# A recurrent scan gated by a GLU: x and the weights in four slots of 128 rows, with the halves of the array trading banks between two turns

## The chip, the cores and the metric

One core of a Trainium2 chip. Its engines run side by side: TensorE (PE, with its weight loads as PEld), VectorE (DVE), ScalarE (ACT), GpSimd (POOL) and SyncE (SP, which only issues DMAs here). The metric is the device time in microseconds, as the median of several runs; smaller is better. Matmul results land in PSUM, which has eight banks of 512 fp32 columns; only DVE and ACT copy from there.

## The reference

Tokens S = 2048, width D = 448, hidden width F = 1792, all bf16. The part that matters here:

```python
xn = layernorm(x)                                   # [2048, 448]
Bu = einsum("bld,pd->blp", xn, B_bar)               # complex, B_bar from Lambda, log_dt, B
h  = Lam_bar * h + Bu[:, t, :]                      # scan over 2048 tokens
s  = 2 * einsum("blp,dp->bld", hseq, Cmat).real + xn * Dskip
g  = einsum("bsd,df->bsf", xn, w_gate)
u  = einsum("bsd,df->bsf", xn, w_up)
gl = einsum("bsf,fd->bsd", sigmoid(g) * u, w_down)
out = x + s * silu(gl)
```

## The kernel before, in words

The tokens go in four chunks of 512 (four tiles of 128 each). The width 448 is seven blocks of 64 rows, so it does not fill a whole number of 128-row contractions. The kernel therefore splits PE's array in two halves of 64 rows. For one gate or up unit (`gu_mm`, L800) the upper half contracts all seven blocks for one column block of the weights into one bank, while the lower half does the same for another column block into a second bank. Seven pairs of matmuls make a unit of 2 x 128 columns by 512 tokens:

```python
T.matmul(bank[0][:, ts], lhsT=w_[0:H, s, ms], rhs=x[0:H, SL[s], ts], start=(s == 0), stop=(s == 6))       # L810
T.matmul(bank[1][:, ts], lhsT=w_[H:P, (s + 1) % 7, ms], rhs=x[H:P, SL[s], ts], ...)                       # L811
```

For this both halves need all 448 rows: `xnT` has seven slots in which the 128 partitions hold 64 rows each for either half, and every row lies there twice. The normalized tile is therefore widened by a copy of its own columns on POOL (in `norm`, L541) before it is transposed; in chunk 0 the tiles are transposed on PE, copied by ACT into four slots (`first_slots`, L593) and the rest is filled by DVE from SBUF (`shift`, L600). Weights `wG` and `wU` lie with one half of their columns in partitions 0 to 63 and the other in 64 to 127, and each DMA fills 64 partitions.

A unit's two banks are one of three `gu` tiles, taken in turn (`next_gu`). After a gate unit ACT takes the tanh of both banks (L844), after an up unit DVE multiplies (L847). The last two banks are `acc0` and `acc1`, for the down and output products and the fourth part of the B product.

The B product (`b_phase`, L873) has four parts for each chunk. It uses three full 128-row contractions (L899, L902) and one half-row pair (L885, L888). Its results go by ACT (L913, L919) to `bus` buffers, and DVE does the scan from them. In chunks 1 to 3 the down products (L1027) and output products (L1046) of earlier chunks stand between the B product's third and fourth part.

The order of each engine is not written out by hand alone: every operation goes with a cost into a planner (`Plan`), PE in the order written, DVE and ACT in the written order in the head (`pl.seq`) and afterwards by due times. DMA issues keep their written order on each queue; eight DMA semaphores are reused in turn, so an issue can wait for an earlier DMA's landing. In the head DMAs are issued from SP, ACT and POOL.

The head: ten warm-up matmuls; statistics of the first tiles on DVE and ACT, roots on ACT (`root`, L485), `norm` on DVE (L531); transposes; then the first two gate units in four pieces of 128 tokens (`last_tile`, L828 and L829), one for each tile as it comes. From there on units have 512 columns; `halves` cuts the first two of chunk 1 in pieces of 256.

Of the kernel before, what the change touches and what calls it, by code (L numbers as in the profile page):

```python
# [15 lines left out]
ENG = mybir.EngineType  # L16

# [229 lines left out]
def kernel(  # L247
# [36 lines left out]
    wgt = {"g": sbt("wG", [7, 896]), "u": sbt("wU", [7, 896])}  # L284
# [3 lines left out]
    xn = [sbt(f"xn{i}", [2 * D]) for i in range(NXN)]  # L288
    SL = [4 * s % 7 for s in range(7)]
    xnT_raw = [sbt(f"xnT{i}", [7 * L]) for i in range(3)]  # L290
    xnT = [flat(t[:], 7, L) for t in xnT_raw]
# [6 lines left out]
    bT6 = sbt("bT6", [4, P])  # L298
# [48 lines left out]
    gu = [pp.tile([P, 2, 512], FP32, name=f"gu{i}") for i in range(3)]  # L347
    acc = [pp.tile([P, 512], FP32, name=f"acc{i}") for i in range(2)]
# [17 lines left out]
    def load_w(eng, k, half, b, r=(), rate=105e3, land=0.0):  # L366
        m0, m1 = BLK[k][b]
        ps = slice(half * H, half * H + H)
        c0 = half * 896
        load(eng, [("w", k, half, m) for m in range(m0, m1)], H * 7 * (m1 - m0) * P * 2,  # L370
             wgt[k][ps, :, m0 * P:m1 * P],
             wsrc[k][:, c0 + m0 * P:c0 + m1 * P].rearrange("(s p) f -> p s f", p=H), cost=0.65, r=r, rate=rate, land=land)

    def load_w0(eng, half, part, r=(), land=0.0):
        ps = slice(half * H, half * H + H)
        s0, c0 = (1 - half if part == "A" else half), half * 896
        n = 4 - s0
        load(eng, [("w", "g", half, m, part) for m in range(2)], H * n * 2 * P * 2, wgt["g"][ps, s0:7:2, 0:2 * P],
             wsrc["g"][:, c0:c0 + 2 * P].rearrange("(s p) f -> p s f", p=H)[:, s0:7:2, :], cost=0.5, r=r, rate=400e3, land=land)

    def wkeys(k, m, part=None):
        if k == "u" or m > 1:
            return [("w", k, 0, m), ("w", k, 1, m)]
        if part == "b":
            return [("w", k, 0, m, "A"), ("w", k, 1, m, "A")]
        return [("w", k, h, m, q) for h in range(2) for q in "AB"]
# [14 lines left out]
    def load_p(eng, k, r=()):  # L401
# [3 lines left out]
    load_x(2, 1, "SP", land=3.7)  # L405
    load_x(1, 1, "ACT", land=3.5)
    add("ACT", 0.05, lambda: A.preload_act_table_set("sqrt_and_others"), w=["sqrttab"], lat=1.3, chain=True)
    load_x(3, 1, "ACT", land=4.3)
    load_w0("SP", 0, "A", land=5.7)
    load_w0("ACT", 1, "A", land=5.9)  # L410
    load_w0("SP", 0, "B", land=6.4)
    load_w0("SP", 1, "B", r=[("x", 0)], land=6.6)
# [5 lines left out]
    load_w("SP", "g", 0, 1, rate=400e3, land=8.5)  # L418
    load_w("SP", "g", 1, 1, rate=400e3, land=9.5)
    load_w("SP", "g", 0, 2, rate=400e3, land=11.0)  # L420
    load_w("SP", "g", 1, 2, rate=400e3, land=12.4)
    load_x(4, 2, land=13.6)
    load_x(6, 2, land=15.1)
# [7 lines left out]
    add("POOL", 0.15, lambda: G.memset(flat(g_raw[:, 512:2048], 3, 512)[:, :, D:512], 0.0),  # L431
        w=[("xnw", t) for t in (1, 2, 3)])
    load_w("SP", "u", 0, 0, rate=400e3, land=16.3)
    load_w("SP", "u", 1, 0, rate=400e3, land=18.2)
    load_w("SP", "u", 0, 1, rate=400e3, land=19.4)
    load_w("SP", "u", 1, 1, rate=400e3, land=20.5)
    load_w("SP", "u", 0, 2, rate=400e3, land=21.6)
    load_w("SP", "u", 1, 2, rate=400e3, land=22.7)
# [9 lines left out]
    def bn(t):  # L448
        b = t % 3
        add("DVE", 0.56 if t < TPC else 0.6, lambda: V.bn_stats(out=bst[b][:], in_=x_all[:, t, :]),  # L450
            r=[("x", t)] + ([("xnT", 0, 3, "a")] if 3 < t < 8 else []), w=[("bst", b)])
# [74 lines left out]

    def norm(t):
        b, o = xkey(t), xbuf(t)
        if t < TPC:
            s1, op0 = (nmf[:, 1, :], ALU.add) if t == 1 else (mvf[:, t, 0:1], ALU.subtract)  # L530
            add("DVE", 0.33, lambda: V.tensor_scalar(out=o[:, 0:448], in0=x_all[:, t, :], scalar1=s1,  # L531
                                                     scalar2=rsd[:, t, :], op0=op0, op1=ALU.mult),
                r=[("x", t), ("mv", t), ("rs", t)], w=[("xn", b)])
        else:
            add("ACT", 0.65, lambda: A.activation(o[:, 0:448], x_all[:, t, :], ACT.Identity,  # L535
                                                 bias=nmr[:, t, :], scale=rsd[:, t, :]),
                r=[("x", t), ("rs", t), ("nm", t)], w=[("xn", b)])
        n = H if t < TPC else D
        if 0 < t < TPC:
            return  # L540
        add("POOL", 0.25 if n == H else 0.6, lambda: G.tensor_copy(out=o[:, D:D + n], in_=o[:, 0:n]),  # L541
            r=[("xn", b)], w=[("xnw", b)])

    def skip_row(t):
        b, q, o = xkey(t), t % NXD, xbuf(t)
        add("DVE", dve2(448), lambda: V.tensor_tensor(out=xd[q][:], in0=o[:, 0:448], in1=dbc[:], op=ALU.mult),
            r=[("xn", b), "dbc"], w=[("xd", q)])
# [3 lines left out]
    def next_acc():  # L551
        a = acc_n[0] % 2
        acc_n[0] += 1
        return a

    def xkeys(c):
        return [("xnT", c % 3, j) for j in range(TPC)]

    def pe_transpose(t, parts, between=None):
        b, js, o = xkey(t), slice(t * P, t * P + P), xbuf(t)  # L560
        tp = {}
        for lo, hi, key, bank, eng in parts:
            for s in range(lo, hi):
                tp[s] = flat(bank.bitcast(BF16)[:, 0:(hi - lo) * P], hi - lo, P)[:, s - lo, :]

        def f():
            for s in (4, 5, 6, 0, 1, 2):
                c0 = s * P if s < 4 else H + (s - 4) * P
                T.transpose(tp[s], o[:, c0:c0 + P], ident[:, :])
        add("PE", 0.64 if t < 2 else 0.34, f, r=[("xn", b), "ident"], w=[p[2] for p in parts])  # L570
        add("PE", 0.1 if t < 2 else 0.06, lambda: T.transpose(tp[3], o[:, 384:512], ident[:, :]), r=[("xnw", b)], w=[parts[-1][2]])
        for i, (lo, hi, key, bank, eng) in enumerate(parts):
            if i and between:
                between()
            n = (hi - lo) * P
            w = [("xnT", 0, t, h) for h in (("a" if lo == 0 else "b") if len(parts) == 2 else "ab")]
            src = flat(bank.bitcast(BF16)[:, 0:n], hi - lo, P)
            if eng == "ACT":
                add("ACT", 0.05 + n / 1120.0, lambda src=src, lo=lo, hi=hi: A.copy(out=xnT[0][:, lo:hi, js], in_=src), r=[key], w=w)
            else:  # L580
                add("DVE", 0.07 + n / 1600.0, lambda src=src, lo=lo, hi=hi: V.tensor_copy(out=xnT[0][:, lo:hi, js], in_=src), r=[key], w=w)

    def first_slots(t, key, bank, eng):
        b, js, o = xkey(t), slice(t * P, t * P + P), xbuf(t)
        tp = flat(bank.bitcast(BF16)[:, 0:512], 4, P)

        def f():
            for s in range(3):
                T.transpose(tp[:, s, :], o[:, s * P:s * P + P], ident[:, :])
            T.transpose(tp[:, 3, :], o[:, 384:512], ident[:, :])  # L590
        add("PE", 0.24, f, r=[("xn", b), ("xnw", b), "ident"], w=[key])
        cost, e = (0.51, A.copy) if eng == "ACT" else (0.39, V.tensor_copy)
        add(eng, cost, lambda: e(out=xnT[0][:, 0:4, js], in_=tp), r=[key], w=[("xnT", 0, t, "a")])  # L593

    def shift(t, half, eng):
        js = slice(t * P, t * P + P)
        dst, src = ((slice(0, H), slice(4, 7)), (slice(H, P), slice(0, 3))) if half == 0 else (
            (slice(H, P), slice(3, 7)), (slice(0, H), slice(0, 4)))
        cost, e = (0.45, A.copy) if eng == "ACT" else (0.32, V.tensor_copy)
        add(eng, cost, lambda: e(out=xnT[0][dst[0], dst[1], js], in_=xnT[0][src[0], src[1], js]),  # L600
            r=[("xnT", 0, t, "a")], w=[("xnT", 0, t, half)])
        if half == 0:
            add("NONE", 0.0, lambda: None, r=[("xnT", 0, t, 0), ("xnT", 0, t, 1)], w=[("xnT", 0, t, "b")], lat=0.0)

    def dma_transpose(t):
# [4 lines left out]
        tload([k + ("a",), k + ("b",)], xnT[c % 3][:, :, js], o, P * 1792, r=[("xn", b), ("xnw", b)] + al)  # L610

    def xr(c, lo=0, hi=TPC):
        return [("xnT", c % 3, j, h) for j in range(lo, hi) for h in "ab"]
# [50 lines left out]
    def silu_table():  # L664
        add("ACT", 1.3, lambda: A.preload_act_table_set("silu_and_others"), r=[("sd", t) for t in range(4)] + [("xnT", 0, 3, "a"), "pv0"], w=["silutab"])
# [519 lines left out]
    for i in range(4, 13):  # L1185
        gu_step(0, i)
# [82 lines left out]
```

## Time and profile before

| what | value |
|---|---|
| median of 3 runs | 183.17 us (183.04 to 183.57) |
| the profiled execution's own time | 183.15 us |
| its span, first to last instruction | 181.4 us |
| around the span | 1.75 us |
| granted TensorE clock | 1.00 |
| PE / DVE / ACT / POOL busy | 176.9 / 166.5 / 97.4 / 35.2 us |

How to read it: the page's first part gives busy time, share of the span and number of instructions of each engine. The second cuts the span in 40 slices of 4.5 us and gives tenths of busy time in each, and what the DMAs moved. A timeline line gives start and duration in microseconds, engine, line of the kernel, operation, what it writes and reads, and in brackets how long the engine was idle before and what ended that. In a line of the waits view stand the total, the number and the longest of the waits of one line for another. PE's duration of a matmul is its whole passage, not its spacing; the spacing is read from starts.

### The profile page before, as it was taken

How to read it: one execution, taken by the hardware profiler on the slowest of the kernel's cores; microseconds unless marked ns; L12 is line 12 of the kernel's file. 1: busy time of each engine (PE TensorE's matmuls, PEld its weight loads, DVE VectorE, ACT ScalarE, POOL GpSimd, SP SyncE). 2: the span in 40 equal slices, each digit the busy share in tenths (PEclk: the TensorE clock that was granted, in tenths of full speed). 3: DMA queues.
4: the chain of work that ended last, by engine and by line, in shares of the span. 5: the costliest groups of instructions: out<-in, count | busy, mean ns of one | idle time of the engine just before them, and what ended most of it. 6: DMA issues, size and time to landing. Idle time of an engine off the chain costs nothing.

```text
span 181.4 us, 3610 instructions
## 1 busy us (share of the span) xinstructions
PE 176.9 (98%) x1404; PEld 89.0 (49%) x1411; DVE 166.5 (92%) x294; ACT 97.4 (54%) x160; POOL 35.2 (19%) x93
## 2 busy tenths in 40 slices
PE   8999999999999999999999999999999999999993
PEld 2755555654544444455554444444555444455552
DVE  3768889999989999999999999999999999999772
ACT  4899998867699984464155543348110533411100
POOL 6464483000018785000004100000000000000000
PEclk9999999999999999999999999999999999999999
DMA  4999999998000390000004900002000000002111
GB/s 122 245 224 228 183 157 203 291 217 248 4 0 0 62 145 0 0 4 0 0 2 91 131 9 0 4 0 73 3 4 0 25 27 28 1 0 76 50 62 47
DMA packets 30852, 13.43 MB, mean 74 GB/s; under 512 B 19441, under 2 KB 30834, under 8 KB 30834
## 3 DMA queue, kind: packets, MB, share of 16 engines
q1 hardware_dynamic: 30208, 12.83, 35.0%
q10 hardware_dynamic: 562, 0.36, 0.7%
q8 instruction: 11, 0.18, 0.5%
q14 instruction: 7, 0.06, 0.1%
q0 software_dynamic: 64, 0.00, 0.0%
HBM read 6.77 MB, written 1.84 MB: 47 GB/s over the span
## 4 chain that ended last, share of the span: by engine, by line
PE 94%; DMA 2%; DVE 1%; ACTq 0%; issue 0%; ACT 0%; DVEq 0%
PE gu L810 36%; PE gu L1027 15%; PE acc L1046 11%; PE acc L1027 9%; PE gu L899 8%; PE gu L811 8%; DMA wG<-in_B_w_gate_dram 2%; PE acc L902 2%; PE gu L885 2%; PE gu L828 2%; PE acc L810 1%; ACTq L357 0%; DVE o_t L1088 0%; PE gu L829 0%; DVE o_t L1082 0%
## 5 line engine op out<-in xcount | busy, mean ns | idle before, releaser
L810 PE MATMUL gu<-xnT,wU 64*128 64x512 bf16 x196 | 45.8, 376 | 0.0
L811 PE MATMUL gu<-xnT,wU 64*128 64x512 bf16 x196 | 45.8, 376 | 0.0
L811 PE MATMUL gu<-xnT,wG 64*128 64x512 bf16 (+1 forms) x189 | 41.3, 360 | 0.0
L810 PE MATMUL gu<-xnT,wG 64*128 64x512 bf16 (+1 forms) x189 | 41.3, 360 | 0.0
L844 ACT ACTIVATE sig<-gu 128x1024 f32<-128x1024 f32 x21 | 21.3, 1019 | 24.7 <-PE gu L811 20.2
L1027 PEld LDWEIGHTS <-hF 128*128 128x128 bf16 x224 | 21.9, 98 | 20.6
L1027 PE MATMUL gu<-wd,hF 128*128 128x448 bf16 x140 | 28.0, 352 | 0.0
L810 PEld LDWEIGHTS <-wG 64*128 64x128 bf16 x196 | 18.3, 94 | 17.5
L810 PEld LDWEIGHTS <-wU 64*128 64x128 bf16 x196 | 18.4, 94 | 17.1
L847 DVE SCALAR_TENSOR_TENSOR hF<-sig,gu 128x1024 bf16<-128x1024 f32 x21 | 25.4, 1210 | 0.7 <-ACT sig L844 0.4
L1046 PE MATMUL acc<-cT,hT 128*128 128x448 bf16 (+2 forms) x119 | 22.9, 337 | 0.0
L966 DVE TENSOR_TENSOR_SCAN wv<-c_r,st,z 128x512 bf16<-128x512 f32 x18 | 22.8, 1271 | 0.0
L811 PEld LDWEIGHTS <-wU 64*128 64x128 bf16 x196 | 18.4, 94 | 5.2
L1033 ACT ACTIVATE g_t<-gu 128x448 bf16<-128x448 f32 x10 | 5.4, 540 | 27.7 <-PE gu L1027 16.8
L811 PEld LDWEIGHTS <-wG 64*128 64x128 bf16 x196 | 18.3, 94 | 2.3 <-DMA wG<-in_B_w_gate_dram 0.3
L1027 PE MATMUL acc<-wd,hF 128*128 128x448 bf16 x84 | 16.9, 352 | 0.0
L1046 PEld LDWEIGHTS <-hT 128*128 128x128 bf16 x126 | 11.7, 98 | 9.9 <-issue 0.4
L899 PE MATMUL gu<-xnT,bT 128*128 128x512 bf16 x65 | 15.3, 379 | 0.4
L913 ACT CAST bus<-gu 128x1024 bf16<-128x1024 f32 x12 | 12.0, 1011 | 5.9 <-PE gu L885 5.3
L541 POOL COPY xn<-xn 128x448 bf16<-128x448 bf16 x12 | 7.5, 626 | 28.9 <-ACT xn L535 28.7
L919 ACT CAST bus<-acc 64x256 bf16<-64x256 f32 (+1 forms) x24 | 8.7, 368 | 5.1 <-PE acc L902 4.8
L450 DVE BATCH_NORM_STATS2 bst<-x_all 128x6 f32<-128x448 bf16 x11 | 6.4, 612 | 4.8 <-DMA x_all<-in_A_x_dram 4.8
(162 smaller groups left out, 262.4 us busy)
## 6 DMA issues: line engine op xcount, KB each, us to landing
wd<-in_B_w_down_dram SPq DMA_DIRECT2D x2, 784.0 KB, 6.7
out_dram<-o_t SPq DMA_DIRECT2D x14, 112.0 KB, 1.7
wU<-in_B_w_up_dram SPq DMA_DIRECT2D x4, 224.0 KB, 8.8
x_all<-in_A_x_dram SPq DMA_DIRECT2D x2, 448.0 KB, 4.1
wG<-in_B_w_gate_dram SPq DMA_DIRECT2D x2, 336.0 KB, 7.1
wU<-in_B_w_up_dram SPq DMA_DIRECT2D x2, 336.0 KB, 7.8
wG<-in_B_w_gate_dram SPq DMA_DIRECT2D x2, 224.0 KB, 5.4
x_all<-in_A_x_dram SPq DMA_DIRECT2D x2, 224.0 KB, 7.9
```

Source lines behind the costliest of these rows:

```text
L450: add("DVE", 0.56 if t < TPC else 0.6, lambda: V.bn_stats(out=bst[b][:], in_=x_all[:, t, :]), r=[("x", t)] + ([("xnT", 0, 3, "a")] if 3 < ...
L541: add("POOL", 0.25 if n == H else 0.6, lambda: G.tensor_copy(out=o[:, D:D + n], in_=o[:, 0:n]), r=[("xn", b)], w=[("xnw", b)])
L810: T.matmul(bank[0][:, ts], lhsT=w_[0:H, s, ms], rhs=x[0:H, SL[s], ts], start=(s == 0), stop=(s == 6))
L811: T.matmul(bank[1][:, ts], lhsT=w_[H:P, (s + 1) % 7, ms], rhs=x[H:P, SL[s], ts], start=(s == 0), stop=(s == 6))
L844: add("ACT", act(1024), lambda: A.activation(th, gu[a][:], ACT.Tanh, scale=0.5), r=[("gu", a)], w=[tk])
L847: add("DVE", dve1(1024), lambda: V.scalar_tensor_tensor(out=ho, in0=th, scalar=1.0, in1=gu[a][:], op0=ALU.add, op1=ALU.mult), r=[("gu", a) ...
L899: T.matmul(gu[slots[pt]][:, i, :], lhsT=bT[:, kt, i, pt * P:pt * P + P], rhs=x[:, kt, :], start=(first and kt == 0), stop=(not first and k ...
L913: add("ACT", act(1024), lambda: A.copy(out=bus[u][:], in_=gu[slots[pt]][:]), r=key(pt), w=[("bus", u)])
L919: add("ACT", 0.36, lambda ns=ns, d=d, q=q, l=l, i=i: A.copy(out=bus[u][d, l, ns], in_=acc[a3[i]][q, 0:256]), r=[("acc", a3[i])] + ([("bus" ...
L966: dve(1.194, lambda k=k: V.tensor_tensor_scan(out=wv[:, k, :], data0=rb, data1=z[:, k, :], initial=(st[pt][:, k, :] if c else 0.0), op0=AL ...
L1027: T.matmul(d, lhsT=hF[c % 2][:, m, h, js], rhs=wd[:, ft, :], start=(ft == 0), stop=(ft == FT - 1))
L1046: T.matmul(y, lhsT=hT[c % 2][:, hm, js], rhs=cT[:, cm, c0:c1], start=(i == 0 and not skip_on_pe), stop=(i == 6))
```

## The change

x and the weights are laid out in four slots of 128 rows: rows 0, 128, 192 and 320 onward. The upper half of the array then has blocks 0, 2, 3 and 5 of the seven, the lower half blocks 1, 3, 4 and 6; block 3 is in both. Each half multiplies its own rows for both column blocks. A unit is one pair for block 3 (`z_mm`: each half for its own bank), three pairs of the first turn (`ph_mm` with i = 0, same banks) and three of the second turn (i = 1), in which the halves trade banks. Before a half writes a bank that the other half wrote, PE waits for that product. The second turn of a unit is put behind the first two pairs of the next one (`run_unit`, `flush`); in the pieces (`both`) two units alternate. The ring gets `acc` as a fourth tile. The B product is done in the same way, with no 128-row matmuls. The POOL copies and the DVE shifts go; chunk 0's tiles 1 to 3 are transposed by each half for itself (`row_transpose`), with one copy on ACT and one on DVE. `norm` writes 512 columns in two overlapping pieces of 256. Weight DMAs fill 128 partitions with rows of 512 or 768 columns; the first weights come in four DMAs, two from SP and two from ACT. The rows of `wd` are taken in another order to match.

```diff
-    wgt = {"g": sbt("wG", [7, 896]), "u": sbt("wU", [7, 896])}
+    wgt = {"g": sbt("wG", [4, F]), "u": sbt("wU", [4, F])}
-    xn = [sbt(f"xn{i}", [2 * D]) for i in range(NXN)]
+    xn = [sbt(f"xn{i}", [4 * P]) for i in range(NXN)]
+    LO, UP = (slice(0, H), (0, 1, 3), 2), (slice(H, P), (0, 2, 3), 1)
+    gu = [pp.tile([P, 2, 512], FP32, name=f"gu{i}") for i in range(4)]
+    acc = [gu[3][:, i, :] for i in range(2)]
...
+    load_w0("SP", 0)
+    load_w0("ACT", 1)
+    load_w0("SP", 2)
+    load_w0("ACT", 3)
...
     def norm(t):
-        n = H if t < TPC else D
-        if 0 < t < TPC:
-            return
-        add("POOL", 0.25 if n == H else 0.6, lambda: G.tensor_copy(out=o[:, D:D + n], in_=o[:, 0:n]),
...
+    def row_transpose(t, keys, banks):
+            for s in range(4):
+                for h, (hs, _, _) in enumerate((LO, UP)):
+                    T.transpose(tp[h][:, s, :], o[hs, s * P:s * P + P], ident[hs, hs])
+    def row_copy(t, h, key, tp):
+        js = slice(t * P + h * H, t * P + h * H + H)
+        eng, cost, e = (("ACT", 0.33, A.copy), ("DVE", 0.25, V.tensor_copy))[h]
...
+    def row_mm(bank, h, fn, start=False):
+        pe_n[0] += 1
+        other = None if start else wrote.get((bank, 1 - h))
+        if start:
+            wrote.pop((bank, 1 - h), None)
+        if other and other[0] > seen[0]:
+            tc.add_manual_dep(T.nop().ins, other[1].ins.name, SYNC, reason="other rows' product in this bank")
+            seen[0] = other[0]
+        wrote[bank, h] = (pe_n[0], fn())
+    def z_mm(u, start):
+            for b, (hs, _, s) in enumerate((LO, UP)):
+                row_mm(banks[b], b, lambda: T.matmul(out[b], lhsT=w(b, hs, s), rhs=x(b, hs, s), start=start, stop=False), start)
+    def ph_mm(u, i, qs=(0, 1, 2), start=False, stop=False):
+            for q in qs:
+                for h, (hs, ss, _) in enumerate((LO, UP)):
+                    b = 1 - h if i else h
+                    row_mm(banks[b], h, lambda: T.matmul(out[b], lhsT=w(b, hs, ss[q]), rhs=x(b, hs, ss[q]),
+                                                         start=start and q == 0, stop=stop and q == 2), start and q == 0)
+    def flush():
+        if open_unit:
+            u, done = open_unit.pop()
+            ph_mm(u, 1, stop=True)
+            done()
+    def run_unit(u, done):
+        n0 = 1 if u[6] == L else 3
+        z_mm(u, True)
+        ph_mm(u, 0, range(n0))
+        flush()
+        if n0 < 3:
+            ph_mm(u, 0, range(n0, 3))
+        open_unit.append((u, done))
+    def both(us, first=False, last=False, between=None):
+        if first is None:
+            z_mm(us[0], True)
+            flush()
+            z_mm(us[1], True)
+        for u in us:
+            ph_mm(u, 0, start=first is True)
+        if first is not None:
+            for u in us:
+                z_mm(u, False)
+        if between:
+            between()
+        for u in us:
+            ph_mm(u, 1, stop=last)
...
     def b_phase(c, mid=None):
-        for pt in (3, 0, 1):
-            add("PE", ..., lambda pt=pt: fulls(pt, False), ...)
-            evac(pt)
+        for pt in (3, 0, 1, 2) if c else (0, 1, 3, 2):
+            run_unit(unit(pt), lambda pt=pt: evac(pt))
         if mid:
             mid(...)
+            flush()
-        add("PE", 1.29, lambda: fulls(2, True), ...)
-        add("PE", 0.22 + SW, lambda: halfrows(2, False), ...)
-        evac(2)
```

## The prediction

> **What bounds the kernel now.** I read four views in this order. First the page's busy line and slices, to see which engine is full:
>
> ```profile
> PE 176.9 (98%) x1404; PEld 89.0 (49%) x1411; DVE 166.5 (92%) x294; ACT 97.4 (54%) x160; POOL 35.2 (19%) x93
> PE   8999999999999999999999999999999999999993
> GB/s 122 245 224 228 183 157 203 291 217 248 4 0 0 62 145 0 0 4 0 0 2 91 131 9 0 4 0 73 3 4 0 25 27 28 1 0 76 50 62 47
> ```
>
> PE is full in every slice but the first and last. A busy PE need not be fast, so the second view is PE's waits:
>
> ```profile
> PE gu L444 <- PEq L1253: 0.8, 1, 0.8
> PE gu L829 <- DMA wG<-in_B_w_gate_dram: 0.3, 1, 0.3
> ```
>
> After the first product PE waits once, 0.3 us for weights. Third, PE's timeline at the end of the gate/up work, for the spacing:
>
> ```profile
> 155.71 0.38 PE L810 MATMUL gu<-xnT,wU 64*128 64x512 bf16 x1
> 155.71 0.38 PE L811 MATMUL gu<-xnT,wU 64*128 64x512 bf16 x1
> 155.92 0.38 PE L810 MATMUL gu<-xnT,wU 64*128 64x512 bf16 x1
> ...
> 156.35 0.38 PE L810 MATMUL gu<-xnT,wU 64*128 64x512 bf16 x1
> ...
> 156.66 0.93 PE L1046 MATMUL acc<-cT,hT 128*128 128x448 bf16 x4
> ```
>
> L810 and L811 start together: the two halves run as a pair, and pairs follow each other every 0.215 us. From the last pair to the first 128-row matmul there is 0.31 us: 0.095 more, which I call a **switch**. From 10.34 us, where the 512-column units begin, to the last matmul, the starts hold nothing else beyond matmul counts times spacing (some records are missing). So the kernel is a head of 10.34 us and then PE's list. Only the head, the length of the list, or a new PE wait can move the time. Fourth, the head's timeline:
>
> ```profile
> 1.74 0.41 ACTq L357 DMA_DIRECT2D x_all<-in_A_x_dram  x1
> 2.19 0.70 ACTq L357 DMA_DIRECT2D wG<-in_B_w_gate_dram  x1
> 3.81 0.30 ACT L485 ACTIVATE sdb<-mvf,epsc 128x1 bf16<-128x1 f32 x1 [0.82 <-DVE mvf L456]
> 4.37 0.36 DVE L531 TENSOR_SCALAR g_t<-x_all,mvf,rsd 128x448 bf16<-128x448 bf16 x1
> 5.23 0.36 DVE L581 COPY xnT<-acc 128x384 bf16<-128x384 bf16 x1
> 5.64 0.22 PE L828 MATMUL gu<-xnT,wG 64*128 64x128 bf16 x1
> 6.11 0.23 PE L829 MATMUL gu<-xnT,wG 64*128 64x128 bf16 x1 [0.25 <-DMA wG<-in_B_w_gate_dram]
> 6.98 0.59 ACT L593 COPY xnT<-gu 128x512 bf16<-128x512 bf16 x1 [0.42 <-PE gu L590]
> 10.34 0.38 PE L810 MATMUL gu<-xnT,wG 64*128 64x512 bf16 x1
> ```
>
> To be seen: the chain root (3.81), norm (4.37), transpose, copy (5.23), product. From 6.11 to 10.34 PE is nearly closed: 55 pairs of 128 columns at 0.056 (starts at 8.50, 8.55 and 8.61 in the same view) and 12 transposes at about 0.056 make 3.75 of the 4.23 us.
>
> **The change part by part.**
>
> *PE's list after the head.* Gate/up: seven pairs for each unit before and after (one that both halves do of the middle 64 rows, and 3 + 3 turns). The B product was six 128-row matmuls and one pair; it becomes seven pairs, at the same spacing. Two switches go, those of chunk 0's B product, where nothing of 128 rows is left: 2 x 0.095 = **-0.2 us**. Weight loads do not bind: in the 128-column stage a pair with its two loads took 0.056.
>
> *The new wait at each turn.* In the changed program as built, 89 weight loads on PE wait for PE's own semaphore: a half may enter a bank only after the other half's last product there is complete. Behind such a load everything on PE is queued. Price: ACT at L844 in the window around 70 us was waiting for PE, the unit's last pair started at 69.74 and ACT at 70.16, so a 512-column product is out 0.42 us after its start. In a steady unit two pairs stand between (z and the first turn's first pair of the next unit), so the matmul behind the wait is due at 3 x 0.215 = 0.645. That leaves 0.22 for a load of 0.09. I take **0**; the bounds are no gain and, if each of the some 62 steady turns lost as much as a switch, 62 x 0.095 = 5.9 us. Nearest is the row of 0.42, so 0. In the half-tile units (`halves`) there is less between: one 256-column pair after chunk 0's B product (due at 0.33, wants 0.43: 0.1), one after each 256-column z (0.1), and small change at the end of chunk 3: **+0.25** in all, 0 to 0.5.
>
> *The head.* Three things count here.
>
> (a) ACT now issues the fourth piece of the first weights, and as built that issue waits for the semaphore of x tile 1 before it can take it over. x tile 1 is issued at 1.30 and lands 2.5 us later (the page's DMA issues: x_all on ACTq, median 2.5), about 3.85. The issue takes 0.4 (row at 1.74). The root of tile 0 is the next instruction on ACT, so it starts at 4.3, not 3.81. Behind it hang norm, transpose, copy and PE: **+0.5**. The norm writes 512 columns instead of 448 (+0.05), the copy takes 512 rather than 384 (+0.1) and waits for four transposes, not three (+0.05). The distance from root to first product was 5.64 - 3.81 = 1.83, so the first product starts at 4.3 + 1.83 + 0.2 = 6.35. Before, PE was held by the weights until 6.11, so only 0.25 of this shows. The fourth piece, issued at 3.9 behind two larger transfers on SP's queue, lands at 6.1 to 6.5 and is wanted two pairs later: no wait of its own.
>
> (b) Self-waits with little between. In a 128-column tile the order is turn 1 of units 0 and 1, z of 0, z of 1, turn 2 of 0. After z of 0 only one pair stands between: due 0.11 after its start, ready at 0.25 to 0.3 (L590 starts at 6.73, ACT at 6.98). I take 0.16, and 0.05 for the passage to the next tile. Three tiles pay the first (in tile 1 the transposes of tile 3 stand between), two the second: about 0.6.
>
> (c) Tile 1's columns. Before, its copy ran beside tile 0's second half. Now the transposes follow all of tile 0, then ACT copies one half (256 columns: 0.37, as L919), and as built the DVE copy of the other half waits for ACT (about 0.25), and PE for both. Tile 0 ends at 6.35 + 14 x 0.056 + 0.16 = 7.3; transposes to 7.5; out at 7.7; ACT to 8.1; DVE to 8.4; PE resumes at 8.45, with 0.7 idle (tile 2's transposes take 0.2 of that hole). Tile 1: 8 pairs, tile 3's transposes, 6 pairs: 1.0, to 9.45. Tiles 2 and 3: 0.05 + 0.78 + 0.16 each, to **11.45**.
>
> So the 512-column units begin at 11.45 instead of 10.34: **+1.1**. Gone in exchange are DVE's six shifts (L600, 1.9 us) and ACT's wide copies. Neither engine ended a PE wait, so that is worth nothing itself; nor are POOL's copies (7.5 us) and the smaller DMA transposes, as those columns lay ready before PE came.
>
> *Weights.* One seventh more bytes, in 128 partitions instead of 64. In the slices, the 64-partition loads ran at 224 to 245 GB/s, the down weights (128 partitions, slice 8) at 291. I take the latter: no wait. At 228 GB/s, with the lag of about 2 us that the landings showed, the third gate block would come at 14.3 for a need at 13.8, and I allow 0.5. [...]
>
> *Buffers.* Two units are open at once, and acc joins the ring as a fourth: usually 3.45 us from a unit's end to the bank's next start (3.0 before), but 1.94 where only three may be used, and the fourth unit of chunks 2 and 3 must now leave its bank within 2.7 us; before, DVE did it at 88.3, ten us late. Copies out took 1.5 to 2.7 us from the unit's end. I take 0; up to 1.5 if DVE comes late.
>
> **Sum**, on the profiled execution of 183.15 us (span 181.4 and 1.75 around it; the median is 183.17): 183.15 + 1.1 - 0.2 + 0.25 = **184.3 us**. Without (a), 0.25 less.
>
> **Rivals.**
> *The head closes up.* x tile 1 lands earlier and the copies hide: PE starts near 6.1 and runs 56 pairs and 12 transposes with no hole, 6.1 + 3.1 + 0.7 = 9.9. That is -0.45; with -0.2 and +0.25, 182.75. For it: 0.48 of the old head is waits and switches that could go. Against: ACT's order as built and the DVE-after-ACT copies.
> *The turn's wait bites.* This is the firm slower case: if the release of a waiting load takes over 0.13 us longer than ACT's, each of 62 turns is late; at a switch's 0.095 each, +5.9, 190. Against: the spare 0.22. The trace of before has no PE wait on PE.
> *Late evacuation.* DVE, 100% busy from 80 to 170 us, holds a bank: +1 to 1.5, 185.5. For it: the slack of 1.94 and 2.7 against copies of 1.5 to 2.7. Against: in the old trace PE never waited for DVE.
> *It nets out:* (a) does not show, and the hole before tile 1 shrinks to the 0.2 that tile 2's transposes fill: 184.3 - 0.25 - 0.5 = 183.55. For it: landings move by some tenths. Against: both holes follow from the order as built.
>
> **How the numbers follow.** A measurement of this kernel can tell about 0.3%, 0.55 us. Forecast 0.50; late evacuation 0.11; the turn's wait 0.08; nets out 0.12; the head closes up 0.19. Faster 0.19, same 0.13, slower 0.68. The range takes in the closed head (182.75, and without the half tiles' 0.25, 182.5) and late evacuation with the bounds of the weights and half tiles (186.0); outside lie the turn's wait and tails.
>
> **What would show it.** The first 512-column unit at 11.4 (the closed head: 9.9); tile 0's root at 4.3 behind ACT's DMA issue; PE idle 0.4 to 0.7 between tiles 0 and 1; pairs still every 0.215 across turns; from the first 512-column pair to the end, 171.0 before, 171.1 after. A gap at every turn, or PE waiting for DVE or ACT after 20 us, would make it wrong.

## The result and the profile after

The changed kernel takes **193.84 us** (median of 4 runs, 193.37 to 194.05); the kernel before took 183.19 beside it (183.04 to 183.57). The ratio is 1.0574, with a 95% interval of 1.0548 to 1.0601. The forecast was 184.3 with a range to 186.0: right in sign, wrong in size by 9.5 us. The profiled execution's span is 192.2 us (181.4 before).

The page of the changed kernel, its busy line and two of its slice rows:

```profile
PE 180.2 (94%) x1516; PEld 89.6 (47%) x1516; DVE 163.6 (85%) x291; ACT 96.9 (50%) x158; POOL 27.3 (14%) x76
...
PEclk9859999999999999999999999999999999999999
...
GB/s 147 351 363 209 107 0 110 254 213 226 34 0 0 3 102 7 3 0 0 27 0 27 77 10 0 0 27 24 24 24 5 0 0 0 3 24 72 49 75 50
```

PE is no longer full (94%, was 98%). In the second and third slice the granted clock is 0.8 and 0.5; before, this row was 9 in every slice:

```profile
PEclk9999999999999999999999999999999999999999
```

The loads run at 351 and 363 GB/s where they ran at 245 and 224. The waits of PE, longest first:

```profile
PE gu L791 <- DMA wG<-in_B_w_gate_dram: 2.3, 1, 2.3
PE gu L1017 <- DVE o_t L1039: 2.1, 3, 0.7
PE gu L1015 <- DVE o_t L1039: 1.3, 1, 1.3
PE gu L781 <- DVE hF L844: 0.8, 1, 0.8
```

Before, the longest wait of PE after its first product was 0.3. Now there are one of 2.3 us for weights in the head and, behind the head, five for DVE, at 102, 146, 157, 181 and 186 us. Measured by the gap between starts beyond the usual spacing, those five cost 0.88, 0.88, 0.93, 0.88 and 1.44: 5.0 us. The timeline of the head:

```profile
4.35 0.30 ACT L475 ACTIVATE sdb<-mvf,epsc 128x1 bf16<-128x1 f32 x1 [1.39 <-DMA x_all<-in_A_x_dram]
...
5.87 0.63 DVE L440 BATCH_NORM_STATS2 bst<-x_all 128x6 f32<-128x448 bf16 x1 [0.58 <-DMA x_all<-in_A_x_dram]
...
6.47 0.42 DVE L552 COPY xnT<-gu 128x512 bf16<-128x512 bf16 x1
...
6.95 0.29 PE L791 MATMUL gu<-xnT,wG 64*128 64x128 bf16 x4 [0.52 <-DVE xnT L552]
...
9.52 0.61 PE L791 MATMUL gu<-xnT,wG 64*128 64x128 bf16 x8 [2.28 <-DMA wG<-in_B_w_gate_dram]
```

PE does two pairs at 6.95, then stands until 9.52, because the fourth piece of the first weights, issued by ACT at 3.91, lands at 9.47. Then comes the second loss. In windows of 5 us (columns: window, length, busy time of PE, PEld, DVE, ACT and POOL with their counts, granted clock, DMA share, GB/s):

```profile
5.00:10.00 5.00, 1.59 (x24) 1.16 (x25) 2.35 (x8) 1.62 (x7) 2.12 (x7) 0.83 1.03 356
10.00:15.00 5.00, 4.42 (x92) 3.85 (x88) 1.63 (x6) 2.22 (x5) 1.71 (x5) 0.50 1.08 366
15.00:20.00 5.00, 4.99 (x76) 2.73 (x74) 3.24 (x11) 4.18 (x5) 2.39 (x7) 0.99 1.20 186
```

From 10 to 15 us the clock is 0.50, and pairs of 128 columns follow each other every 0.107 us instead of 0.056. The first 512-column unit begins at 16.32 (10.34 before). So the span's 10.85 us more are 5.98 in the head and 4.87 behind it, and the latter is, within 0.15, the five waits for DVE.

The single stop here was 2.5 us, with three gaps of 0.5 to 0.8 between starts in the 2 us before it. The clock fell at 8.28, while PE still stood; the clock record ahead of that has 1.00 from 4.86 on, and in its 3.41 us PE had been busy for 1.24, so not idle throughout.

### The profile page after: what moved, and what is told of

It reads as the page before. It is cut to its first block, busy times and chain, and to the rows that moved or that the text cites. A ratio compares the mean times of both kernels' runs of the same rounds, so it can differ in the third digit from the quotient of the medians.

```text
span 192.2 us, 3796 instructions
## 1 busy us (share of the span) xinstructions
PE 180.2 (94%) x1516; PEld 89.6 (47%) x1516; DVE 163.6 (85%) x291; ACT 96.9 (50%) x158; POOL 27.3 (14%) x76
## 4 chain that ended last, share of the span: by engine, by line
PE 82%; DVE 8%; DMA 6%; issue 1%; SPq 0%; ACTq 0%; ACT 0%; DVEq 0%
PE gu L791 45%; PE gu L998 21%; PE gu L1017 9%; PE gu L781 7%; DMA wG<-in_B_w_gate_dram 3%; DVE wv L937 2%; DMA out_dram<-o_t 2%; DVE o_t L1039 2%; DMA x_all<-in_A_x_dram 1%; DVE hF L844 1%; DVE tb L952 1%; DVE o_t L1059 0%; DVE o_t L1041 0%; DVE o_t L1040 0%; DVE ta L951 0%
## 5 line engine op out<-in xcount | busy, mean ns | idle before, releaser
L791 PE MATMUL gu<-xnT,wG 64*128 64x512 bf16 (+2 forms) x432 | 49.5, 341 | 3.4 <-DMA wG<-in_B_w_gate_dram 2.3
L791 PE MATMUL gu<-xnT,wU 64*128 64x512 bf16 x336 | 47.6, 376 | 0.0
L998 PE MATMUL gu<-wd,hF 128*128 128x448 bf16 x224 | 44.5, 353 | 0.0
L998 PEld LDWEIGHTS <-hF 128*128 128x128 bf16 x224 | 21.7, 98 | 21.2 <-issue 1.3
L791 PEld LDWEIGHTS <-wG 64*128 64x128 bf16 x432 | 20.4, 99 | 21.7 <-DMA wG<-in_B_w_gate_dram 2.5
L844 DVE SCALAR_TENSOR_TENSOR hF<-sig,gu 128x1024 bf16<-128x1024 f32 x21 | 25.4, 1208 | 2.1 <-PE gu L791 1.9
L1017 PE MATMUL gu<-cT,hT 128*128 128x448 bf16 (+2 forms) x126 | 23.6, 332 | 2.1 <-DVE o_t L1039 2.1
L791 PEld LDWEIGHTS <-wU 64*128 64x128 bf16 x336 | 16.3, 94 | 19.1 <-PE gu L791 0.2
L791 PE MATMUL gu<-xnT,bT 64*128 64x512 bf16 (+1 forms) x192 | 21.6, 350 | 0.0
L1039 DVE TENSOR_TENSOR o_t<-gu,xd 128x448 bf16<-128x448 f32 x15 | 9.3, 620 | 8.7 <-PE gu L998 4.5
L791 PEld LDWEIGHTS <-bT 64*128 64x128 bf16 x192 | 9.0, 94 | 9.5 <-issue 1.1
L781 PE MATMUL gu<-xnT,wG 64*128 64x512 bf16 (+2 forms) x72 | 11.6, 344 | 0.8 <-DVE hF L844 0.8
L528 ACT ACTIVATE xn<-x_all,nmr,rsd 128x512 bf16<-128x512 bf16 x12 | 9.3, 806 | 3.6 <-DVE xd L533 3.3
L781 PE MATMUL gu<-xnT,wU 64*128 64x512 bf16 x56 | 10.6, 376 | 0.0
```

The lines of the kernel that those rows point to most:

```text
L528: add("ACT", 0.7, lambda: A.activation(o, x, ACT.Identity, bias=nmr[:, t, :], scale=rsd[:, t, :]), r=[("x", t), ("rs", t), ("nm", t)], w=[ ...
L781: row_mm(banks[b], b, lambda: T.matmul(out[b], lhsT=w(b, hs, s), rhs=x(b, hs, s), start=start, stop=False), start)
L791: row_mm(banks[b], h, lambda: T.matmul(out[b], lhsT=w(b, hs, ss[q]), rhs=x(b, hs, ss[q]), start=start and q == 0, stop=stop and q == 2), s ...
L844: add("DVE", dve1(1024), lambda: V.scalar_tensor_tensor(out=ho, in0=th, scalar=1.0, in1=gu[a][:], op0=ALU.add, op1=ALU.mult), r=gk(a) + [t ...
L998: T.matmul(d, lhsT=hF[c % 2][:, m, h, js], rhs=wd[:, ft, :], start=(ft == 0), stop=(ft == FT - 1))
L1017: T.matmul(y, lhsT=hT[c % 2][:, hm, js], rhs=cT[:, cm, c0:c1], start=(i == 0 and not skip_on_pe), stop=(i == 6))
```

## The experiments

All times are medians beside the kernel before (183.1 to 183.3) on the same chip; each interval is that of the ratio to it. "First unit" is the start of the first 512-column unit, "list" the time from there to the last matmul's start (before: 10.34 and 167.72; changed: 16.32 and 172.60).

### Where the head's 6 us come from

**e1: the fourth piece ahead of the gate blocks.**

```diff
-    load_w0("ACT", 3)
+    load_w0("SP", 3)
```

> The fourth piece of the first weights is issued on SP, ahead of the gate blocks, instead of on ACT. Theory 'queued last': the piece was late (9.47 us) because three larger transfers of SP were issued before it was served; now it lands by about 7, ACT's root of tile 0 starts near 3.9 instead of 4.35, PE never stops between 7.1 and 9.5, the granted clock stays near 1.0, and the first 512-column unit begins at 11.5 to 12 instead of 16.0: about 4.3 us less, 189.5 us. Rival 'the loads are simply slower than thought': the piece still lands after 9 and the time falls by at most 0.5, to 193.3. Rival 'clock': the piece comes early but the clock still falls for some 5 us: about 191.5.

Measured: 191.04 us, ratio 1.043 (1.0384 to 1.0475), 2.8 us less than the changed kernel. All four pieces have landed by 7.10, and PE's wait for weights shrinks to 0.5. So it was the place in the order of issue, not the rate. But the clock still fell for part of the stage (0.83 in 5 to 10 us and 0.82 in 10 to 15, 0.107 us a pair up to 11.5, first unit 13.16): the first theory and the clock's rival are both in part right.

**e5: PE kept busy while it waits.**

```diff
+    def more_warm():
+        for _ in range(10):
+            T.matmul(gu[2][:, 0, :], lhsT=ones[:, 0:P], rhs=ones[:, 0:512], start=True, stop=True)
+    add("PE", 0.0, more_warm, w=uk)
     both(first(0), True)
```

> The changed kernel with ten idle matmuls of 128 rows and 512 columns on PE just ahead of the first product; the planner isn't told and nothing else moves. They fill the time in which PE waits for the fourth piece (6.95 to 9.5 us), 2.15 us at full clock. Theory 'idle PE, slower clock': the granted clock fell to 0.50 in 10 to 15 us because PE stood still before; busy, it stays near 1.0, the 128-column stage takes 3 us less, and the first whole unit begins near 13.5 instead of 16.3: 191 us (190.5 to 191.8). Rival 'the clock falls for what the stage itself does': the stage stays at 0.107 a pair and the time at 193.8 or above.

Measured: 192.28 us, 1.0495 (1.0452 to 1.0539). The same windows of this kernel:

```profile
5.00:10.00 5.00, 4.04 (x42) 1.98 (x43) 2.28 (x8) 1.62 (x7) 2.54 (x8) 1.00 1.05 357
10.00:15.00 5.00, 4.31 (x128) 3.36 (x126) 3.01 (x8) 3.58 (x6) 1.41 (x4) 1.00 1.08 366
```

The clock stays at 1.00, with the same loads and the same late piece; the first unit begins at 14.31, 2.0 earlier. The time falls by 1.6, less than the expected 2.8: PE still waits 0.8 for the piece, and one of the four runs lost the clock again (mean 0.99, 193.1 us; the others 1.00, 191.3 to 192.8). So it is the standing that cost the clock here, not the stage.

### Where the 4.9 us behind it come from

**e2: the fourth ring unit as two tiles** (with e3: both edits).

```diff
-    acc = [gu[3][:, i, :] for i in range(2)]
+    acc = [pp.tile([P, 512], FP32, name=f"acc{i}") for i in range(2)]
...
+        if a == 3:
+            for i in range(2):   # one copy out for each tile
```

> The fourth ring unit is made of two tiles of one bank each (acc0, acc1), as in the kernel before, instead of two halves of one tile; its copies out are two instructions of 512 columns. Theory 'one tile': DVE's read of a y bank waited for the down product that PE had begun in the other half; apart, the four stalls of PE after 100 us (0.88, 0.88, 0.88, 1.44) go, 4.1 us less, 189.8 us, and the stall of 0.93 before the last two units stays. Rival 'DVE is just late': the same stalls stay within 0.2 each, 193.8 us.

Measured: 193.74 us, 1.0573 (1.0529 to 1.0616): no gain. The first of the changed kernel's five stalls on DVE looks like this:

```profile
102.47 0.10 PEld L1017 LDWEIGHTS <-hT 128*128 128x128 bf16 x1
102.86 0.62 DVE L1039 TENSOR_TENSOR o_t<-gu,xd 128x448 bf16<-128x448 f32 x1 [2.41 <-PE gu L998]
...
103.54 1.49 PE L1017 MATMUL gu<-cT,hT 128*128 128x448 bf16 x7 [0.71 <-DVE o_t L1039]
```

DVE should read an output product that was finished before the down product L998 began, and reads it only when L998, which writes the other half of the same tile, is through: 2.41 idle. PE then waits 0.71 for DVE. With separate tiles the stalls at 102 and 146 are gone, as expected, and that at 157 too, which I had expected to stay. But two others stand at the end:

```profile
PE acc L1024 <- DVE o_t L1048: 1.2, 1, 1.2
PE acc L1026 <- DVE o_t L1048: 1.1, 1, 1.1
```

and the span ends 4.7 us after the last matmul's start instead of 3.3. So the shared tile did stall PE, but another lag of DVE lay behind it.

**e4: the kernel before, with the shared tile alone.**

```diff
-    acc = [pp.tile([P, 512], FP32, name=f"acc{i}") for i in range(2)]
+    acc2 = pp.tile([P, 2, 512], FP32, name="acc2")
+    acc = [acc2[:, i, :] for i in range(2)]
```

> The kernel before, with one edit: acc0 and acc1 are the two halves of one tile. Theory 'one tile': DVE's reads of y in the two alternating banks now wait for the product that follows in the other bank, and PE stalls at the same four places by 0.9 to 1.4 each: 183.2 + 4 = 187.2 us (186 to 188). Rival: the order of reads is set by the banks and not by the tile, and the time stays at 183.2.

Measured: 188.63 us, 1.029 (1.0257 to 1.0324): 5.5 more, from nothing but the way in which two banks are declared. PE's first two waits, and DVE's copy of tile 0 in the head's timeline:

```profile
PE acc L1047 <- DVE o_t L1069: 2.1, 3, 0.7
PE gu L811 <- DVE hF L848: 0.9, 1, 0.9
```

```profile
6.29 0.36 DVE L582 COPY xnT<-acc 128x384 bf16<-128x384 bf16 x1 [1.04 <-PE acc L638]
```

Three stalls of 0.88 stand where the changed kernel has them; 1.1, 0.5 and 0.4 come from copies that fell behind, and 0.9 is the head's. There the same cause is at work: the copy, at 5.23 before, now waits 1.04 for small products of L638 that write the other half of the tile, and the first product comes at 6.70 instead of 5.64. The changed kernel has this wait too: its copy (L552) waited 0.39 for L602 in e1 and 0.48 in e10.

**e3: both edits.**

> Both edits. If the two causes are independent, the savings add: 193.8 - 4.3 - 4.1 = 185.4 us, which is what the prediction's sum gives plus the one stall of 0.93 (184.3 + 0.93). If a third cause is hidden behind them it stays above 187.

Measured: 190.04 us, 1.0368 (1.0327 to 1.0408). The head is nearly as forecast (first unit 11.92, clock 1.00), but the list is 171.02 and its end late, as in e2. A third cause is hidden, as the last sentence of the expectation allows: DVE waits 4.7 + 3.0 us for gate and up products here, 0.3 in the kernel before.

**e7: e3, and the planner told.** Only the order on DVE, ACT and POOL may change.

```diff
+    add("PE", 1.5, lambda: None)
     one(0, 2, "g", slots0[2])
```

> The kernel of both edits (190.04 us) with one more line: the planner is told that the 512-column units begin 1.5 us later than it thought (10.45 planned, 11.92 in the trace); no instruction is added or taken away, only the order on DVE, ACT and POOL may change. Theory 'stale order': DVE's instructions stand in an order that fits the planned time, so it waited 7.7 us in all for gate/up products that came later than planned (0.3 in the kernel before), fell behind, and PE paid at the end (1.30 + 1.41 in two stalls, and 1.3 more after the last product). Told the truth, those 4.0 go: 186.0 us (185 to 187). Rival 'DVE is simply full': its work starts later and nothing can be won by order: 189.5 or more.

Measured: 186.45 us (185.40 to 187.81), 1.0182 (1.0118 to 1.0245): 3.6 less than e3. The profiled execution is the slowest of the four: its pairs of 128 columns are 0.107 us apart up to 13.4, as at a clock of 0.50 in the changed kernel, though its windows give 1.00 from 0 to 20 us, and its first unit begins at 14.15. The lists compare the order alone: 167.60 against 171.02, 3.4 less, and PE has no late stall. DVE's waits for products, in e3 and then in e7:

```profile
DVE hF L853 <- PE gu L791: 4.7, 9, 1.9
...
DVE hF L846 <- PE acc L791: 3.0, 3, 1.8
```

```profile
DVE hF L846 <- PE acc L791: 3.4, 1, 3.4
...
DVE hF L853 <- PE gu L791: 2.3, 7, 0.5
```

Their sum falls from 7.7 to 5.7. What changes more is the place: one wait of 3.4 near 20 us, where DVE has time, in place of several in the middle. From 40 to 120 us DVE is busy 78.7 of 80 us in the kernel before, 74.0 in e3 and 77.2 in e7.

**e8 and e9: the kernel before, PE 1.6 us late, untold and told.** Seven idle matmuls ahead of the first whole unit, with cost 0 or 1.5 for the planner.

> The kernel before with seven idle matmuls of 128 rows and 512 columns (7 x 0.215 and a switch, 1.6 us) on PE ahead of the first whole unit; the planner isn't told, so the orders of all other engines stay. Theory 'stale order': the time rises by more than the 1.6 us that PE is late: DVE waits for gate/up products, and PE stalls on DVE later: 183.1 + 1.6 + 1 to 4 = 186 to 189 us. Rival: everything shifts by 1.6 and nothing more: 184.7 us.

> The same seven matmuls, with their 1.5 us given to the planner. Theory 'stale order': the order of DVE fits again, and only the delay itself is left: 184.7 us (184.3 to 185.2), less than the untold one by what that lost beyond 1.6. Rival 'DVE is simply full': told or not is the same within 0.5.

Measured: 184.85 (1.0115, 1.0067 to 1.0164) and 185.11 us (1.0109, 1.0092 to 1.0126). The rival held both times: the order of the kernel before bears a late PE, and telling it wins nothing. DVE takes the delay in one wait of 3.4 us (e8) or 3.0 (e9) near 20.

**e10 and e11: the changed kernel told of 5.6 us**, as it stands and with separate tiles.

> The changed kernel; the planner alone is told that the whole units begin 5.6 us later than it thought (10.45 planned, 16.3 in the trace). No instruction is added. Theory 'stale order': DVE's order fits, its waits for gate/up products shrink, the stall of 0.93 before the last two units and half of the last one (1.44) go, while the stalls of 0.88 that the shared tile makes stay: 191.5 to 192.5 us. Rival 'order is nothing' (as the delayed kernel before showed: 184.85 untold, 185.11 told): 193.8.

> Separate tiles for the two acc banks, and the planner told of the 5.6 us. Separate tiles alone gave nothing (193.74), as DVE's lag brought two other stalls (1.31 and 1.41) and a later end (4.65 us after the last product instead of 3.3). Theory 'two causes that hide each other': with both gone 189.7 us (189 to 190.5). Rival: 193 or more.

Measured: 198.54 (1.0831, 1.0783 to 1.0879) and 194.89 us (1.0627, 1.0596 to 1.0658): both worse than untold. In e11 the stalls after 100 us did go. But the new order put ACT's other work ahead of a tanh, and PE stood 3.3 us at 22; e10's longest wait:

```profile
PE gu L781 <- ACT hF L841: 3.1, 1, 3.1
```

My theory in its plain form, "tell the planner the true time and the loss goes", has fallen. What is left: the order decides some 3 to 5 us, and neither kernel's order follows from the delay in a simple way.

**e16: more work for DVE alone,** in the kernel before. One multiply in chunk 1 is done five times.

```diff
-        dve(dve2(1024), lambda: V.tensor_tensor(out=ta[:], in0=b, in1=cosb, op=ALU.mult), ...)
+        def more():
+            for _ in range(5 if (c, pt) == (1, 0) else 1):
+                V.tensor_tensor(out=ta[:], in0=b, in1=cosb, op=ALU.mult)
+        dve(dve2(1024), more, ...)
```

> The kernel before, with one multiply of DVE in chunk 1 (1024 columns, about 0.6 us) done five times instead of once: 2.4 us more work on DVE near 85 us, unknown to the planner; PE's list is the same. Theory 'DVE has no slack between 30 and 170 us': its chain ends 2.4 later, the 1.2 us that it waits for PE at 170 are used up, and PE stalls for the rest: 1.2 us more, 184.4 us (184.0 to 185.5). Rival 'PE alone bounds the kernel': no change, 183.2 us.

Measured: 184.96 us, 1.0107 (1.0082 to 1.0132), 1.8 us more. The multiply before, the five of this run, and PE's wait:

```profile
60.88 0.81 DVE L959 TENSOR_TENSOR ta<-bus,cosT 128x1024 bf16<-128x1024 bf16 x1
```

```profile
60.83 3.95 DVE L961 TENSOR_TENSOR ta<-bus,cosT 128x1024 bf16<-128x1024 bf16 x5
```

```profile
PE gu L810 <- DVE hF L847: 1.3, 2, 1.0
```

The added work is 3.1 us, not 2.4, and it stands at 61 us, not 85. PE at 98% was not the only bound: of these 3.1 us DVE takes up some 1.5, and PE stands for the rest, 1.19 at 65 us and 0.43 at 106. The time came out as expected, but not by the expected path: PE was to stall at the end and DVE's wait of 1.2 for PE near 171 to be used up, and that wait is still there (1.2 at 172). So DVE time that is lost does turn into stalls of PE. That would account for e2, where taking away one stall uncovered the next; it is not shown that e2's two stalls at the end came about in this way.

### The turn's wait, and what is left

**e6: one pair between the turns instead of two.**

```diff
-        n0 = 1 if u[6] == L else 3
+        n0 = 0 if u[6] == L else 3
```

> The changed kernel, but in whole units the second turn of the unit before is done right behind the new unit's middle pair: one pair of 512 columns stands between the two turns instead of two. In the traces the load that waits for the other half's product goes 0.23 to 0.245 us after that product's last column (128-column tiles: 0.285 from its start; 256-column halves: 0.35). At 512 columns that is 0.213 + 0.245 = 0.46 from its start, and with one pair between the next is due at 0.43: 0.03 lost at each of some 62 turns, +1.9, 195.7 us (with two pairs, due at 0.645, nothing). Rival 'a waiting load costs a fixed tenth or more whatever stands between': two pairs would have shown it too; here +6 or more, 200 us.

Measured: 198.05 us, 1.0809 (1.079 to 1.0828). Its steady units:

```profile
66.64 0.38 PE L781 MATMUL gu<-xnT,wU 64*128 64x512 bf16 x2
66.87 0.82 PE L791 MATMUL gu<-xnT,wG 64*128 64x512 bf16 x6
67.53 0.81 PE L791 MATMUL gu<-xnT,wU 64*128 64x512 bf16 x6
```

From L781 to the turn behind it there are 0.228 us, 0.012 beyond the spacing, and 0.010 more a pair later: 0.022 for each turn, some 1.4 us for 62 turns, near the 1.9 expected. The other 2.8 us I did not expect: 1.3 of them are longer stalls on DVE, among them one of 1.85 at 179 us, and 1.2 a later end (4.5 us after the last matmul's start instead of 3.3). With two pairs, as changed, the turns cost nothing: L781 of successive units starts at 66.07, 67.58 and 69.09, 1.51 us for seven pairs, 0.216 each.

**e12: tile 1's transposes and copies inside tile 0's product**, on e7 with 1.1 told.

```diff
-    both(first(0), True)
-    tp = {1: row_transpose(1, uk, ub)}
-    row_copy(1, 0, uk[0], tp[1][0])
...
+    def second():
+        tp[1] = row_transpose(1, uk, ub)
+        row_copy(1, 0, uk[0], tp[1][0])
...
+    both(first(0), True, between=second)
```

> The kernel of both edits and the told planner (median 186.45, best 185.4), with tile 1's transposes and copies moved into tile 0's product, between the middle pairs and the second turn, as tile 3's stand in tile 1's. The hole of 0.84 between tiles 0 and 1 should shrink to 0.4: 185.0 us where the clock holds; a slower clock in the head adds up to 2. Not below the kernel before (183.1): its head is still about 1 longer. Rival: the copies wait for each other as before and PE waits at the same place: 185.4 or more.

Measured: 185.64 us, 1.0138 (1.009 to 1.0185); 184.9 in the runs with clock 1.00 and 186.4 to 186.6 in those with 0.99. The hole shrinks from 0.84 to 0.43, the first unit begins at 11.39, and the list is 167.61. Of the 1.6 us that its span has over the kernel before's, 1.05 are the head and 0.7 the end.

**e13, e14, e15: the middle pair ahead, a fourth output buffer, both**, on e12.

```diff
         for u in us:
-            ph_mm(u, 0, start=first is True)
-        if first is not None:
-            for u in us:
-                z_mm(u, False)
+            if first is not None:
+                z_mm(u, first is True)
+            ph_mm(u, 0)
...
-    NGT, NO = 5, 3
+    NGT, NO = 5, 4
```

> The kernel of e12 (184.86 to 186.57 us), with a unit's middle pair ahead of its first turn in the 128-column tiles and in the second half of the half tiles, so that three or four pairs stand between a half's entry into a bank and the other half's last product there, instead of one. DVE's order is the same. Theory 'a load waits 0.23 to 0.245 us after the last column, less what stands between': the waits of 0.17 to 0.24 in four tiles and of 0.12 in two half tiles go down to 0.06 or nothing: 0.6 to 0.8 less, 184.1 us where the clock holds. Rival 'a change of half costs that in any place': the same as e12.

> The kernel of e12 with four output buffers instead of three (the planner then orders DVE anew as well). In e12's trace DVE waits 2.1 us at 175.5 for the store of an earlier output, and the span ends 4.0 us after the last product instead of 3.3. Theory 'the buffer': that wait goes, and 0.7 with it: 184.2 us where the clock holds. Rival 'DVE is behind for its work': the end stays 4.0 after the last product, 184.9.

> Both. By the sum 183.5 us where the clock holds in the head, 185 where it falls: the head is still some 0.6 longer than the kernel before's (183.26), the list 0.3 shorter. Not distinguishable from the kernel before, or up to 1% slower.

Measured: 185.90 (1.0136, 1.0104 to 1.0168), 186.20 (1.0153, 1.0124 to 1.0182) and 185.51 us (1.0129, 1.0111 to 1.0146). By time none is told from e12. In the traces e13's waits in the 128-column tiles go from 0.15 to 0.18 down to 0.11 or less, and one of the two of 0.12 in the half tiles stays; e14's 2.1 us wait is gone (the view had put it down to a down product; that it goes with a fourth buffer speaks for the store), and the end comes 3.7 us after the last product instead of 4.0, half of what I expected. Their first units began at 12.0 to 12.5, later than e12's. In e13 and e15 the clock fell in the head (0.83 in 5 to 10 us and 0.70); in e14 it stayed at 1.00, but PE waited 0.92 for weights at 7.4. What the head does by chance is larger than either effect. No version beats the kernel before.

## Why the prediction was wrong, by its steps

- **The failed step: "the piece ... lands at 6.1 to 6.5: no wait of its own".** It landed at 9.47. The prediction counted two transfers ahead of it and did not add up the bytes: x tile 3, three first pieces and three gate blocks, 1.42 MB, had been issued and not landed when it was issued at 3.9. With its own 0.13 MB, at the 291 GB/s that the prediction itself took, that makes 5.3 us, 9.2. That it comes so near is in part luck: at the 351 to 363 GB/s of these slices the same bytes would be through by 8.2 to 8.4. Of the head's 5.98 us, e3 and e5 give 2.4 for the wait and 2.0 for the clock; 1.58 remain (e3), against 1.1 forecast.
- **The clock** was in no step. Every price for the 128-column stage was taken at 0.056 a pair; behind a stop of PE it was 0.107 (with PE kept busy, in e5's profiled execution, the clock stayed at 1.00).
- **The second failed step: buffers, "I take 0; up to 1.5".** I saw that `acc` became one tile of the ring, and priced only when its bank comes free, not that a read of one half now waits for a write of the other. 4.9 us stood there: 2.6 are the three stalls of 0.88 (e2, e4). The stalls of 0.93 and 1.44 are put down to DVE's lag; none of the five is left when separate tiles and another order come together (e7, e12). The rival "late evacuation" named the right engine with a price that was too small, and "PE never waited for DVE" in the old trace was no sign of much slack: DVE took up some 1.5 us of added work (e16).
- **The turn's wait at 0** was right, and so was its reason, the two pairs between (e6). The halves' +0.25 measured 0.12 + 0.12. The rival that priced every turn at a switch, 190 us, would have come nearest in time for a wrong reason.
- **The list**: 171.0 to 171.1 forecast from the first whole unit to the span's end. With the stalls gone the list was 167.60 and 167.61 against 167.72 before (e7, e12), so the sum of -0.2 and +0.25 stands within 0.2.
- **The head's parts**: the root started at 4.35 (4.3 forecast) behind ACT's DMA issue, and the hole between tiles 0 and 1 was 0.79 (0.7). The self-waits were 0.15 to 0.18 in each of three tiles (0.16 and 0.05). The first product came at 6.95, not 6.35: x tile 3 landed at 5.85 (4.25 before; 4.81 in e5, with the same issues), its statistics stood on DVE ahead of tile 0's copy, and the piece hid this. Without them the copy would still have waited for L602 in the shared tile, as in e1 and e10.
- **Weights**: no wait for them after the head, at 351 to 363 GB/s, more than the 291 I took. That the 128 partitions are the cause is not shown: the rows of these loads also grew, from 512 or 768 bytes to 1024 or 1536.

What stays open: why the order planned for the changed kernel loses some 3 us in the middle of DVE's work where that of the kernel before bears the same delay. That order does it is shown (e3 against e7); by which of DVE's instructions was not tried.

## What to carry to other kernels

For a new DMA, add up all bytes issued before it and not yet landed, on every queue, before believing a landing time (here 1.42 MB, and 5.6 us from issue to landing for a piece of 0.13 MB); and where PE will stand as it did here, for 2.5 us, price the work behind it at half clock too (0.107 us a pair instead of 0.056). Declare banks that alternate as tiles of their own: two halves of one tile were one thing to whoever waited for it (5.5 us in e4). An engine as busy as DVE here beside a full PE (78.7 of 80 us) can be a second bound: 3.1 us more work on it made the kernel 1.8 us longer (e16). Test it with idle work on it alone before you price a delay at nothing.

## What the runs showed of the hardware

- The clock fell after a stop of 2.5 us in the changed kernel, and a longer stop did not always bring it down: e10 and e11 both stood 3.3 us, up to 25.7 and 25.4, and in 25 to 30 us the granted clock was then 1.00 in e10 and 0.66 in e11. No run here shows what made the difference. In the clock records, every stretch at 0.50 that begins and ends within a run lasted 3.413 us (e1, e13, e15, e11's second) or 6.827 (the changed kernel, e2, e6, e11's first), twice as long.
- The fourth piece, alone behind x tiles and one other piece on ACT's queue, landed 0.19 us after the last of three gate blocks that SP had issued up to 1.3 us earlier (9.28). Its 128 packets moved from 7.01 to 9.04, while SP's queue moved 0.64 MB, and none of them in the 3.1 us after its issue at 3.91; why they began so late is open. In this head the loads of x and the weights landed in the order of issue from the first at 2.77 to the fourth gate block at 10.55, whichever of the two queues they were on.
- A weight load that waits for the other half's product went 0.22 to 0.245 us after that product's last column, at 128, 256 and 512 columns alike (0.28, 0.35 and, in e6, 0.44 from its start).
